# Attention on one core: two matmuls of ones moved ahead of the first transposition, another count of planned matmul work, and new orders for four engines

## The chip, the core and the metric

The kernel runs on one core of one Trainium2 chip. The core has five engines that run side by side, each through its own list of instructions in order: TensorE (PE, matrix products, with weight loads PEld that overlap them), VectorE (DVE), ScalarE (ACT), GpSimd (POOL) and SyncE (SP), whose list here holds the issues of transfers (DMAs). Engines wait for each other through semaphores. The metric is device time in microseconds, the median of the runs of one kernel.

## The reference

32 heads, 2048 positions, 20 elements a head. Queries and keys are normalised to length one, the logits are scaled by one factor a head, and softmax attention follows:

```python
def setup_inputs():
    ...
    B, H, S, D = 1, 32, 2048, 640
    Dh = D // H
    ...
def reference(q, k, v, t):
    eps = 1e-6
    qn = q / (jnp.sqrt((q * q).sum(axis=-1, keepdims=True)) + eps)
    kn = k / (jnp.sqrt((k * k).sum(axis=-1, keepdims=True)) + eps)
    logits = jnp.einsum('bhqd,bhkd->bhqk', qn, kn) * t[None, :, None, None]
    attn = _softmax(logits, axis=-1)
    return jnp.einsum('bhqk,bhkd->bhqd', attn, v)
```

The cost is the 32 x 2048 x 2048 exponentials: the products have only 20 rows or columns, and all data are 16-bit floats.

## The kernel before

**Units.** A head's 2048 x 2048 logits are cut into 64 units of 128 keys by 512 queries. Two paths turn logits into exponentials.

The first is ScalarE's. TensorE puts a *wave* of two or three units into the accumulator psA (L903 for products on 21 rows of the array, two or three side by side; L910 for products on 64 rows, two side by side), and one ACTIVATE (L998) turns the wave into 16-bit exponentials in the ring p_ring. Waves of two and three units alternate in two halves of psA, so TensorE can write one while ScalarE reads the other. There are 1204 such units in 482 waves. ScalarE takes them strictly in their number's order.

The second is VectorE's. TensorE puts four units, as two products on 64 rows (L915), into psF, and one pass on VectorE (L1059) makes of them integers whose two 16-bit halves, read as floats, are rough exponentials. Three shifted copies of that tile (the same integers plus a constant) are made either by VectorE (L1072, L1074) or by GpSimd with a 64-bit addition (L1026, one or two copies a call). The four versions, weighted, average the error away. There are 211 such tiles.

**The second product.** L931 multiplies exponentials with the values, four units side by side, each on 32 columns of the array, and accumulates in psF. A column of ones in the values yields the softmax's denominator. At a head's end VectorE transposes the sum (L947), divides (L956, L960) and a transfer stores it.

**Preparation of a head.** Transfers load q, k and v; VectorE squares and sums (L743, L746), forms the inverse root (L750 to L772) and scales (L791); SyncE issues a transposing transfer into qkT (L817, named trn), and from there copies: three rotated sets of keys kR (six transfers a head, named rot), two into qP for VectorE's path (named qo) and four into qz for L910 (named qz). The loads are named ldq, ldk and ldv, the stores st. All of them share SyncE's one list, up to six heads ahead of their use.

**The first head** is done apart, to begin early. Matmuls of ones (L832) run on TensorE as soon as the ones are written. Eleven of them exist; nine stand ahead of the first transposition of keys (L865, named tk0), two among the first waves. VectorE squares and sums q and k (L730, L733), forms the inverse root and scales (L854, L858). A combination with constants in the query tile (L635), for which GpSimd makes columns (L628 to L632), precedes this on VectorE. TensorE transposes the keys in two halves (L865), ScalarE and VectorE copy them out (L874, L876), and VectorE transposes the queries (L868). Then come the first waves. Twelve further matmuls of ones (L873) stand between the waves of this stage. Their results are overwritten later.

**The order** is written out by hand in the class Program: four lists of task numbers, PE, DVE, POOL and SP, and replay() puts the engines' tasks in that order. In POOL an H stands for one of VectorE's instructions that GpSimd's additions may not run beside; a plus sign begins an addition, with two numbers when one call makes two copies, and an s behind a number in DVE says that VectorE makes that copy in the form of L1072. Behind the lists stands times(), which plays the order through with planned durations (a matmul that starts before PE_REST counts double), and fill(), which goes through the planned times in windows of TICK = 3.41 us. Where the planned matmul work of a window falls under FILL, it puts a further matmul into the longest planned pause of TensorE in it, if one is long enough: ones by ones at the start (L842), zeros by ones into the running sum later (L839, four small ones). The work of a task is counted in columns of a matmul that fills the whole array:

```python
    TICK = 3.41
    FILL = 4200.0
    FGAP = 0.32
    GAP0, EARLYPE = 0.24, 45.0
...
            if load(x) < F:
...
            qk.rows, qk.work = (64, 256.0 * len(us)) if two else (32, 128.0 * len(us))
```

plan_waits() then derives every semaphore wait from the tasks' dependences, so a new order gets its own waits.

Of the kernel before, what the change touches and what calls it, by code (L numbers as in the profile page):

```python
# [79 lines left out]
class Program:  # L80
# [4 lines left out]
    PE_REST = 7.3  # L85
# [7 lines left out]
    PE = """  # L93
# [139 lines left out]
    def add(self, eng, name, fn, dur, deps=(), pri=0.0, lat=0.0, dma=None):  # L233
        t = Task(eng, name, fn, dur, deps, pri, lat, dma)
        self.tasks.append(t)
        return t
# [230 lines left out]
def bass_standalone__qk_norm__prompt_kernel(  # L467
# [7 lines left out]
    B, H, S, D = q.shape  # L475
# [36 lines left out]
    with ExitStack() as es:  # L512
# [51 lines left out]
        add = prog.add  # L564
# [621 lines left out]
```

## Time and profile before

| What | Value |
|---|---|
| Median of 3 runs | 562.19 us (562.02 to 566.7) |
| The profiled execution's own time | 570.37 us |
| Its span | 568.6 us |
| TensorE's mean granted clock in it | 0.982 |
| Busy: PE, DVE, ACT, POOL | 548.4, 546.8, 549.5, 472.8 us |
| Exponentials on ScalarE, L998 | 482, together 546.4 us |
| GpSimd's additions, L1026 | 360 calls, 452.2 us |
| Matmuls put in by fill(): L842, L839 | 2, and 32 in fours |

The profiled execution is a single one, taken beside the three timed ones. A row of a group reads: line, engine, operation, target and sources, count, then busy time and the mean of one in ns, then the idle time of the engine just before these instructions with what ended most of it. In rows in order of time the first two numbers are the start and the length, and the bracket is the pause before. In a table of stretches PEclk is the share of its full clock that TensorE was granted; before the first record of the clock, at 5.81 us, it stands at 1.00.

### The profile page before, as it was taken

The numbers are of one execution on the slowest core, as the hardware profiler recorded it, in microseconds if no ns is written. First come the engines' busy times: TensorE is split into PE (matmuls) and PEld (weight loads), VectorE is DVE, ScalarE is ACT, GpSimd is POOL, SyncE is SP. The second block draws the span as 40 slices with busy tenths as digits, with TensorE's granted clock in tenths as the row PEclk, the third lists the DMA queues.
The fourth block names the chain that finished last, engine by engine and source line by source line (L and its number), as shares of the span: only waits on it lengthen the run. The fifth ranks groups of instructions, "written<-read, shape, count | busy, mean of one in ns | idle before, by whom it ended". The sixth has DMA issues, their size and how long they took to land.

```text
span 568.6 us, 15092 instructions
## 1 busy us (share of the span) xinstructions
PE 548.4 (96%) x6267; PEld 157.8 (28%) x6267; DVE 546.8 (96%) x646; ACT 549.5 (97%) x488; POOL 472.8 (83%) x466
## 2 busy tenths in 40 slices
PE   7999999999999989999999999999999999999997
PEld 2122222222222322222222332223223222223322
DVE  8699999989999999999999999999999999999998
ACT  6699999999999999999999999999999999999995
POOL 6386969799699876988789888798888997989994
PEclk8599999999999999999999999999999999999999
DMA  4436544344334343453433444444254432322100
GB/s 66 61 59 97 65 70 76 59 90 61 59 71 72 65 72 60 70 85 61 74 59 75 74 69 68 71 61 73 61 65 81 65 66 45 57 69 53 29 2 30
DMA packets 196229, 36.47 MB, mean 64 GB/s; under 512 B 171769, under 2 KB 196161, under 8 KB 196161
## 3 DMA queue, kind: packets, MB, share of 16 engines
q1 hardware_dynamic: 196016, 35.43, 38.7%
q8 instruction: 49, 0.80, 0.6%
q14 instruction: 20, 0.16, 0.1%
q10 hardware_dynamic: 144, 0.08, 0.1%
HBM read 7.87 MB, written 2.62 MB: 18 GB/s over the span
## 4 chain that ended last, share of the span: by engine, by line
ACT 70%; PE 20%; DVE 5%; SPq 2%; POOL 2%; issue 1%; DMA 0%; POOLq 0%
ACT p_ring L998 70%; PE psF L931 11%; PE psA L903 3%; PE psF L915 2%; PE psA L910 2%; DVE dx L1059 2%; SPq L567 2%; DVE dx L1072 2%; POOL dx L1026 1%; PE psF L873 1%; DVE oT L947 0%; DMA qP<-qkT 0%; DVE rs_sum L746 0%; DVE o_stage L960 0%; PE psF L832 0%
## 5 line engine op out<-in xcount | busy, mean ns | idle before, releaser
L998 ACT ACTIVATE p_ring<-psA 128x1024 bf16<-128x1024 f32 x482 | 546.4, 1318 | 9.1 <-PE psA L903 8.3
L1026 POOL INT64_ADD dx<-dx x360 | 452.2, 1275 | 86.4 <-DVE qkn L791 27.9
L1059 DVE TENSOR_SCALAR dx<-psF 128x1024 int32<-128x1024 f32 x211 | 256.5, 1216 | 14.3 <-PE psF L915 13.9
L931 PE MATMUL psF<-dx,vph 128*32 128x512 bf16 (+1 forms) x2532 | 221.0, 399 | 0.1
L1072 DVE TENSOR_SCALAR dx<-dx 128x1040 int32<-128x1040 int32 x163 | 198.6, 1225 | 0.8
L931 PE MATMUL psF<-p_ring,vaug 128*32 128x512 bf16 x1204 | 109.0, 386 | 0.1
L903 PE MATMUL psA<-qkT,kR 21*128 21x512 bf16 x639 | 99.5, 390 | 6.6 <-ACT p_ring L998 4.3
L931 PE MATMUL psF<-dx,vaug 128*32 128x512 bf16 (+1 forms) x844 | 82.9, 397 | 0.0
L931 PEld LDWEIGHTS psF<-dx,vph 128*32 128x32 f16 x2532 | 57.0, 95 | 86.5 <-issue 54.5
L910 PE MATMUL psA<-qz,kR 64*128 64x512 bf16 x305 | 62.8, 385 | 2.6 <-ACT p_ring L998 2.3
L915 PE MATMUL psF<-qP,kR 64*128 64x512 bf16 x296 | 58.3, 390 | 1.5 <-DVE oT L947 1.1
L903 PEld LDWEIGHTS psA<-qkT,kR 21*128 21x128 bf16 x639 | 24.2, 91 | 96.4 <-ACT p_ring L998 88.6
L931 PEld LDWEIGHTS psF<-p_ring,vaug 128*32 128x32 bf16 x1204 | 28.8, 95 | 42.9 <-issue 28.5
L903 PE MATMUL psA<-qkT 21*128 21x512 bf16 x177 | 35.9, 393 | 1.7 <-ACT p_ring L998 1.3
L931 PEld LDWEIGHTS psF<-dx,vaug 128*32 128x32 bf16 x844 | 21.3, 95 | 30.0 <-issue 20.2
L910 PEld LDWEIGHTS psA<-qz,kR 64*128 64x128 bf16 x305 | 15.6, 93 | 48.2 <-ACT p_ring L998 32.1
L915 PE MATMUL psF<-qP,qkT 64*128 64x512 bf16 x126 | 24.6, 388 | 1.3 <-DMA qP<-qkT 1.3
L915 PEld LDWEIGHTS psF<-qP,kR 64*128 64x128 bf16 x296 | 14.3, 93 | 38.0 <-DVE dx L1059 14.6
L947 DVE STREAM_TRANSPOSE oT<-psF 128x512 f32<-128x512 f32 x32 | 22.8, 712 | 1.9 <-PE psF L931 1.5
L746 DVE TENSOR_REDUCE rs_sum<-sq 128x64 f32<-128x1280 bf16 (+1 forms) x17 | 23.0, 1351 | 0.1
L910 PE MATMUL psA<-qz,qkT 64*128 64x512 bf16 x83 | 19.9, 386 | 0.0
L903 PEld LDWEIGHTS psA<-qkT 21*128 21x128 bf16 x177 | 8.6, 91 | 28.0 <-ACT p_ring L998 24.9
(71 smaller groups left out, 147.2 us busy)
## 6 DMA issues: line engine op xcount, KB each, us to landing
kR<-qkT SPq DMA_DIRECT2D x62, 96.0 KB, 2.2
kR<-qkT SPq DMA_DIRECT2D x62, 64.0 KB, 2.0
qk_sb<-in_k_dram SPq DMA_DIRECT2D x32, 80.0 KB, 2.3
vaug<-in_v_dram SPq DMA_DIRECT2D x32, 80.0 KB, 3.5
out_dram<-o_stage SPq DMA_DIRECT2D x32, 80.0 KB, 1.9
qk_sb<-in_q_dram SPq DMA_DIRECT2D x124, 20.0 KB, 2.5
qz<-qkT SPq DMA_DIRECT2D x104, 21.0 KB
qP<-qkT SPq DMA_DIRECT2D x62, 32.0 KB, 1.9
```

Source lines behind the costliest of these rows:

```text
L567: return add(eng, name, lambda e, tk: e.dma_start(dst, src), dur, deps, pri, lat=lat, dma=key)
L746: sums.append(dv("sum", lambda e, tk, i=i, m2=m2, src=src: e.tensor_reduce(rs["sum"][:, 2 * R * i:2 * R * i + m2], src, AXIS_X, ALU.add), ...
L873: warm.append(add("PE", "warm", lambda e, tk: e.matmul(psO[0], ones[:, 0:128], ones[:, :], start=True, stop=True), PE_MM, [tk_], -198))
L903: return eng.matmul(dst, k_of(h, c, (rho - g) % 4, ps), qkT[h % NT][ps, 0:512], tile_position=(32 * g, 0))
L910: return eng.matmul(dst, k_of(h, c, (rho - g) % 4, ps), qz[h % NZ][ps, g % 2, :], tile_position=(64 * b, 0))
L915: return eng.matmul(dst, k_of(h, c, dl, ps), qP[h % NT][ps, :], tile_position=(64 * b, 0))
L931: last = eng.matmul(psO[h % 2][32 * g:32 * g + 32, :], w_of(g), rhs_of(g), start=start, stop=False, skip_group_check=True, tile_position=( ...
L947: trO[h] = add("DVE", f"tr{h}", lambda e, tk: e.transpose(oT_all[:, so, :, :].rearrange("p r d -> p (r d)"), psO[h % 2]), 0.63, [lambda: p ...
L998: act[w] = add("ACT", f"exp{w}", lambda e, tk: e.activation(p_ring[:, p0 * 512:p0 * 512 + n], psA[:, slot * WAVES[0] * 512:slot * WAVES[0] ...
L1026: return lambda e, tk: e.int64_add(rows(1), rows(0), PHASE_W[c - 1] * 0x100000001)
L1059: return add("DVE", name, lambda e, tk: e.tensor_scalar(dst[:, o + 2 * w0:o + 2 * (w0 + n)].bitcast(I32), psF[:, prog.pair_of[j] + w0:prog ...
L1072: return e.tensor_scalar(gapped(be).bitcast(I32)[:, :, 0:PAD], dx[:, bx:bx + TILE].bitcast(I32), float(PHASE_W[i]), None, ALU.add)
```

## The change

- PE_REST, up to which planned matmuls count double, goes from 7.3 to 6.0 us.
- The first transposition waits for all eleven first matmuls of ones, and the list has all eleven ahead of it.
- A unit of a three-row wave (L903) counts 84 instead of 128 columns in fill(): 512 columns on 21 of 128 rows. The products themselves stay as they are.
- The four lists are new. Tasks are the same, but for one shifted copy that moves from VectorE (162 instead of 163 in the form of L1072) to GpSimd (460 copies in 352 calls instead of 459 in 360). They were planned with transfers that land later than those assumed for the old ones.

In the new lists the head of the kernel reads as follows. TensorE: eleven of ones, the two halves of the transposition, wave 1, wave 0, the first product for VectorE's path, then waves and ones. VectorE: the memsets, with two moved behind the combination of L635 and one moved ahead of the ones, the same chain up to the copy L876, then the qP product and the first tile's L1059 ahead of the second head's squares. SyncE: the same first eight issues, then the three transposing transfers of the first head in a row.

```diff
-    PE_REST = 7.3
+    PE_REST = 6.0
...
     PE = """
-84 83 81 86 80 82 78 79 85 109 110 235 120 237 117 115 282 240 113 121 242 88 245 122 114 118 112 248 291 119 87 250 116 111 300 253 244 256 309 252
...
+87 82 81 86 79 88 83 80 84 85 78 109 110 237 235 282 121 240 118 120 114 242 245 122 119 112 117 248 291 115 250 116 300 253 113 111 256 290 287 244
...
+0 8 4 43 55 9 76 10 95 98 97 99 100 101 102 103 105 106 107 108 124 134 61 283 144 145 146 147 148 93 149 150 92 151 94 152 60 292 286 301 294s 310
...
+H 45 5 44 H 6 49 51 3 H 52 27 46 50 48 53 47 54 H H H 56 H H H H 7 H 57 19 H H H H 58 H H 35 20 66 59 28 36 67 21 72 11 29 H H H 37 73 30 62 68 22 38
...
-            tk1 = add("PE", "tk0", lambda e, tk: tmm(e, psA[:, 2048:2560], kx[:, 0:512], 0, 2), 0.15, [nk1, z_id] + warm[:9], -201)
+            tk1 = add("PE", "tk0", lambda e, tk: tmm(e, psA[:, 2048:2560], kx[:, 0:512], 0, 2), 0.15, [nk1, z_id] + warm[:11], -201)
...
-            qk.rows, qk.work = (64, 256.0 * len(us)) if two else (32, 128.0 * len(us))
+            qk.rows, qk.work = (64, 256.0 * len(us)) if two else (32, 84.0 * len(us))
```

More of the change, by code (lines that the diff above doesn't have):

```diff
@@ L160 @@
-695 686 696 685 697 684 698 833 699 700 834 701 916 925 918s 1070 899s 1079 1088 1097 964 1106 965 1115 933 966 1124 1091s 1177 1090s 1186 1107s 1195
-1126s 1204 967 1117s 1188s 1213 1132 1197s 1179s 1222 968 940 969 1133 970 942 971 1134 972 941 973 1472 974 975 1231 1215s 1278 1279s 1287 1281s 1296
-1225s 1305 1239 1280s 1306s 1314 1297s 1323 1324s 1332 1326s 1388 1473 1397 1398s 1406 1340 1407s 1415 956 1341 955 1342 957 1424 1426s 1433 1425s
-1578 1427s 1587 1581s 1596 1579s 1441 1474 1605 1597s 1614 1475 1623 1476 1477 1449 1478 1450 1479 1448 1480 1481 1482 1632 1617s 1685 1635s 1626s
@@ L164 @@
-1694 1640 1686s 1703 1641 1986 1483 1712 1706s 1721 1715s 1730 1987 1739 1642 1786 1733s 1795 1742s 1804 1747 1787s 1813 1814s 1822 1796s 1831 1823s
-1840 1832s 1841s 1893 1988 1464 1465 1463 1902 1894s 1848 1989 1911 1990 1849 1991 1920 1992 1912 1993 1850 1929 1923s 1938 1932s 1947 1949s 2097
-1950s 2106 1955 2115 2107s 2124 1994 1963 1995 1962 1996 1997 2108 2133 2136s 2142 2126s 2193 2145s 2202 2195s 2150 1964 2151 2205 2211 2494 2152 2220
-2214s 2229 2221s 2238 2230s 2247 2294 2248s 2303 2297s 2312 2255 2495 2321 2306 2330 2322s 2339 2332s 2348 2340s 2401 2349s 2496 2410 2497 2419 2356
@@ L168 @@
-2498 2357 2499 2358 2428 2421s 2437 2413s 2446 2430s 2455 2439s 2605 2449s 2614 2458s 2616s 2463 2500 1977 2501 1978 2502 1979 2503 2623 2504 2632
-2625s 2641 2634s 2650 2642s 2651s 2701 2505 3002 2710 2658 3003 2719 2712s 2728 2722s 2737 2487 2470 2659 2485 2472 2660 2486 2730 2471 2746 2738s
-2755 2756s 2804 2758s 2813 2763 2822 2816s 2831 2815s 2840 2823s 2849 2843s 2858 2850s 2909 2859s 2918 3004 2919 2927 2866 2929s 2936 2939s 2945 3005
-2954 3006 2867 3007 2868 3008 2979 3009 2978 3010 2963 2957s 3108 2966s 2948s 3117 2971 3126 3118s 3135 3128s 3144 3011 2980 3013 3012 3153 3138s 3162
@@ L176 @@
-3501 3932 3941 3915s 3950 3944s 3959 3933s 4011 3961s 4020 3960s 4029 3967 4012s 4038 4023s 4047 4041s 4056 4117 4049s 4126 4050s 4135 4144 4064 4138s
+0 8 4 43 55 9 76 10 95 98 97 99 100 101 102 103 105 106 107 108 124 134 61 283 144 145 146 147 148 93 149 150 92 151 94 152 60 292 286 301 294s 310
+284s 319 172 173 174 142 175 143 176 171 177 141 178 293 179 180 285s 295s 374 383 385s 392 327 401 410 206 419 207 519 208 197 209 328 210 329 211
+198 212 170 169 213 199 214 528 421 537 522s 546 531s 555 539s 427 548s 564 547s 567s 556s 615 624 616s 633 627s 626s 572 443 642 444 651 445 434 446
@@ new lines @@
+447 573 448 436 449 435 450 574 451 660 654s 669 670s 770 773s 779 771s 788 677 781s 797 693 806 694 815 824 825s 880 826s 889 890s 898 883s 907 832
+695 696 833 697 685 698 686 699 684 700 834 701 916 925 1070 899s 1079 918s 1088 1097 964 1106 965 1115 933 966 1124 1090s 1091s 1177 1126s 1186 1117s
+1195 967 1107s 1204 1197s 1188s 1213 1132 1179s 1222 968 969 1133 970 942 971 940 972 941 973 1134 974 975 1472 1231 1215s 1278 1225s 1287 1279s 1296
+1281s 1305 1239 1280s 1314 1306s 1323 1473 1332 1324s 1307s 1388 1326s 1397 1398s 1406 1340 1407s 1415 1341 956 1342 1424 1426s 1433 1425s 1578 1427s
@@ new lines @@
+1587 1581s 1596 1579s 1441 957 955 1474 1605 1597s 1614 1475 1623 1476 1450 1477 1478 1479 1480 1448 1481 1449 1482 1632 1617s 1685 1626s 1694 1687s
+1640 1686s 1703 1641 1483 1986 1712 1706s 1721 1715s 1730 1987 1739 1642 1786 1733s 1795 1742s 1804 1747 1787s 1813 1814s 1822 1796s 1831 1832s 1840
+1824s 1893 1841s 1988 1902 1894s 1848 1989 1911 1990 1962 1991 1465 1849 1992 1464 1993 1912 1920 1463 1850 1994 1929 1923s 1938 1932s 1947 1949s 2097
+1950s 2106 1955 2115 2107s 2124 1995 1963 2108 1964 1997 1996 2133 2136s 2142 2135s 2193 2145s 2202 2195s 2150 2494 2205 2151 2211 2152 2220 2214s
@@ new lines @@
+2229 2221s 2238 2247 2230s 2294 2248s 2303 2297s 2312 2255 2321 2330 2322s 2339 2332s 2495 2348 2340s 2349s 2401 2496 2410 2497 2419 2356 2498 2357
+2499 2358 2500 1977 2501 2428 2421s 2437 2413s 2446 2430s 2455 2439s 2605 2458s 2614 2449s 2616s 2463 2502 1979 1978 2503 2623 2504 2632 2625s 2641
+2634s 2650 2642s 2651s 2701 2471 2505 3002 2710 2658 3003 2719 2712s 2728 2722s 2737 2472 2470 2659 2746 2738s 2755 2758s 2756s 2804 2660 2731 2487
+2486 2813 2763 2822 2816s 2831 2815s 2840 2823s 2849 2843s 2858 2850s 2909 2859s 2918 3004 2919 2927 2866 2929s 2936 2939s 2945 3005 2954 3006 2867
@@ new lines @@
+3007 2978 3008 2485 3009 2868 3010 2963 2948s 2957s 3108 2966s 3117 2971 3126 3128s 3135 3118s 3144 3011 2979 3012 3013 3153 3138s 3162 3147s 3218
+3156s 3227 3165s 3236 3170 3229s 3245 3238s 3254 3171 2980 2995 2994 2993 3172 3263 3257s 3312 3248s 3321 3313s 3330 3271 3504 3339 3331s 3348 3505
+3357 3366 3340s 3417 3350s 3426 3360s 3435 3419s 3444 3374 3428s 3453 3438s 3462 3447s 3471 3456s 3506 3598 3464s 3474s 3607 3601s 3479 3507 3616 3508
+3488 3509 3375 3510 3511 3486 3512 3487 3513 3376 3514 3625 3627s 3634 3618s 3643 3644s 3652 3653s 3708 3709s 3717 3660 3719s 3726 3735 3729s 3744
@@ L177 @@
+3738s 3753 3661 3515 3662 3800 3809 3755s 3818 3761 3812s 3827 3801s 3836 3845 3821s 3854 3830s 3905 3855s 3914 3846s 3923 3862 3863 3502 3503 3501
+3932 3941 3915s 3950 3944s 3959 3933s 4011 3961s 4020 3960s 4029 3967 4012s 4038 4023s 4047 4041s 4056 4049s 4117 4050s 4126 4135 4144 4064 4138s
 4136s 4153 4156s 3864 4119 4154 4065 4155 4066 4161 4162 4163
@@ L184 @@
-+644 +652 +662 +661 +672 +653v,663v +671 453 +772 +782 +780 +790 +789 H +798 463 +799 +791,800 +808,817 +807,816 +809 +818 +827 +882 +881 +892 +891 H
-H H H H H H H H H H H +910 +900 +908 +926,917 +901 +909 +927 +1072 703 +919 H +928 +1073 +1082 +1080 H +1081,1099 717 +1089,1071 +1098,1116 +1127
-+1108 +1125 +1118,1109 +1100v,1196 +1205 +1178 +1180,1189 +1206v,1187 H H H H H H H H H H H H H H +1198 +1223 +1207v,1232 +1234,1216 +1233 +1224 977
-+1214 991 +1298 +1288 +1290,1308 +1289 +1316,1307 +1315,1299v +1317 +1334 +1325 +1333 +1389,1335v +1391,1400 +1390,1399 +1408 H H H H H +1417 1005
@@ L192 @@
-+2213,2222 +2223,2232 1999 +2239 +2231 +2250,2241 +2249,2240 +2296,2305 2013 +2295,2313 +2304 H +2323 +2324 +2315 +2331,2314v +2341 +2333,2342 +2351 H
-+2403,2350 +2402,2411 2027 H H H H +2404 +2420,2412v +2422,2431 +2429 +2448 +2438 +2456,2447 +2440 +2457 +2607 +2606,2615 2041 H H H H H H H +2617 H
-+2626 +2624 +2608,2635 +2643 +2633 +2644 +2653 +2652 H H +2704 +2702 +2713 +2703 2507 +2720 +2711 +2729,2721v H H H H H H H H H +2731 +2740 +2748
-+2739 +2749v,2747 +2757 +2806 +2807v,2805 +2825 +2814 +2824 +2834 +2832 +2841 +2842,2833 +2852 2521 +2851 +2860 +2912 +2861 H H +2910,2920v +2928
@@ L196 @@
-+2921v,2911v +2930 +2938 +2946,2937 H H H H H H H H H +2947,2956 +2965 +2964,2955 +3111 +3109 2535 +3110 +3119 +3129,3120 +3127,3136 H H H H +3145
-2549 +3155,3137 +3154,3146v +3164 +3219,3163 +3230 3015 +3220v,3228 +3239,3221 +3237,3246 H H H H H +3256 +3255 +3266 +3247 +3265 +3264 +3322 +3314
-3029 H +3333 +3332,3341 +3315,3324 +3323v,3349 +3342 +3369 +3358 +3367 +3351 +3368 +3359v,3427 +3420 +3429 3043 +3446 +3436,3418 +3455 +3437
-+3445,3463 +3454 H +3465 +3473 +3472 +3599 +3608 +3610 +3600v,3609v H H H H H H H H H H H H +3619 3057 +3628 +3617,3626 +3635 +3636 +3646 +3637 +3655
@@ new lines @@
+12 74 23 64 70 31 75 65 24 13 69 H 25 32 33 126 14 34 39 125 71 63 128 127 129 40 15 H H H H H H H H H H H 41 16 42 H 130 +303 +304 +312 +302 154 H 17
++320 H H H H H H H H H H H 26 H 18 +313 +322 +321v,311 +376 +375 +384 +386 182 +393 +377 +403 H +411,402 +394,412 H H H H H H H H H H H H H H +395 H
++404 +422 +413v,420 +520,529 216 +521 +558 +538 +557 +540 +530 +565 +549 226 +618 +617 +566 +625 +636 +635 H +634 +645 +643 H H H H H H H H H H H H
++644 +652 +653,662 +663,672 +671,772 +661 +780 +782 453 +791 +790 H +789 463 +798,807 +799,808 +817 +827 +800 +881,818v +809 +816 +892 +891,882 H H H
@@ new lines @@
+H H H H H H H H H +910 +909 +917 +926 +908 +901 +900 +928 703 +919 +927 H +1080 +1071,1089 +1081 H +1100 +1072v,1098 +1073 717 +1082v,1125 +1109
++1099,1108 +1180,1127 +1189 +1118 +1205,1116 +1178,1187 +1196,1206v H H H H H H H H H H H H H H +1216,1198 +1223,1207v +1232,1214 +1224,1233 977 +1234
+991 +1288,1297 +1289 +1308,1299 +1298v,1315 +1317,1290 +1335 +1333,1316v +1325 +1334,1390 +1400,1391 +1389 +1399,1408 H H H +1417 +1409 +1418v,1416
++1436 +1434 1005 +1435 +1580 +1588 +1589 +1598 1019 H H H +1599,1590 +1606 +1608 +1607v,1615 H H H H H H H H H H +1624,1616v +1634,1625 +1635 +1633
@@ new lines @@
++1696 +1697 +1688 1485 H H H +1704 +1714 +1705v,1713 +1722,1695 +1723 +1732 H +1724v,1731 +1741 +1740 +1788 +1798,1789 +1797,1806 +1815 +1805,1807v
++1816 +1823 +1834 +1825 +1842,1833 +1843 1499 H +1895 +1904 1513 +1896v,1903 +1905 H H H H H H H H H +1913 H H H +1921 +1914 +1922v,1930 +1939 +1941
++1931,1940 +1948 +2099 +2098 +2100,2109 +2116 1527 H H H H H H +2127,2118 +2126,2117 +2143 +2144 +2134,2125 +2196 +2194 H H H +2203 H 1999 +2204,2213
++2212 +2222 +2231 +2232 +2239,2223v +2249,2240 +2250v,2241v +2305,2296 +2314 +2315 +2304,2295 +2323 +2306 2013 +2313,2324v +2333,2342 +2341 +2331
@@ new lines @@
++2351 H +2350 +2403 +2411,2402 H H H H H H H 2027 +2412v,2404v +2420,2429 +2431,2422 +2447 +2438 +2440 +2448v,2456 +2607,2457 +2606,2615 2041 H H H H
++2617 H +2626,2608 +2633 +2624 +2643 +2635 +2653 +2644 +2652 H H H +2702 +2711 +2704,2713 +2721 2507 +2703 +2729,2720 H H H +2739,2730 +2747
++2740,2749 +2757,2748 H H H H +2806 +2807 +2805 2521 +2825 +2824 +2834 +2832,2814 +2833v,2841 +2851 +2852 +2860 +2861 +2842 +2911 H H +2912 +2910,2928
++2921,2930 +2920,2938 +2937,2946 H H H H H H H H H +2955,2947v +2965 +2956v,2964 +3110 +3111 +3119 2535 +3109,3120v +3129 +3127,3136 H H H H +3145
@@ new lines @@
+2549 +3154,3146v +3155,3137 +3163 +3220,3164 +3219,3228 3015 +3239,3230 +3237 +3221v,3246 H H H H H H +3255 +3256 +3247v,3264 +3265 +3266 +3322 +3315
+3029 H +3323,3332 +3314 +3333v,3324v +3351 +3341 +3342 +3369 +3358 +3349,3367 +3418,3359v +3368v,3427 +3437 +3445,3436 +3420,3429 +3446 3043 +3463
++3454 +3455 H +3473 +3465 +3472,3599 +3600 +3609 +3610 +3608 H H H H H H H H H H H H +3619 +3617,3626 3057 +3628 +3636 +3635 +3637 +3646 +3654,3645
++3655 +3711 +3710 +3718 +3720 3517 +3727 +3728 +3737 +3736 +3745 +3746 H H H +3756 +3747v,3754 +3802 +3811 +3810 +3820 3531 +3819,3803v +3829 +3828
@@ L204 @@
++3837 +3847 +3839 +3856 +3848 +3838 +3906,3857v +3917 +3908 3545 H H H H +3907 +3925 +3926 +3916 +3943 +3952 +3935 +3951 +3924 +3934 +3942 +3953,3962
++4022 +4013 +4030 +4014v,4021 +4040 +4039,4031v +4048 +4032 +4058 +4057 +4118 +4059 +4120,4129 +4137 +4147 +4127,4145 +4146v,4128v H H H H H H H H
 """
     SP = """
[20 rows of a table removed]
[19 rows of a table added]
 """
```

20 lines of the change are left out of this document (removed), and 157 rows, old and new, of tables (PE, SP).

## The prediction

> **What bounds the kernel now.** I read the head of the page first, then ScalarE's groups, then ScalarE's and TensorE's rows in order of time where ScalarE had pauses, and last a table of stretches for the granted clock.
>
> ```profile
> span 568.6 us, 15092 instructions
> ...
> PE 548.4 (96%) x6267; PEld 157.8 (28%) x6267; DVE 546.8 (96%) x646; ACT 549.5 (97%) x488; POOL 472.8 (83%) x466
> ...
> L998 ACT ACTIVATE p_ring<-psA 128x1024 bf16<-128x1024 f32 x482 | 546.4, 1318 | 9.1 <-PE psA L903 8.3
> ```
>
> Three engines stand at 96 to 97%, but only ScalarE (ACT) has a row that cannot shrink: 482 exponentials, 546.4 us, the same count after the change. The span is therefore: time to the first exponential, 546.4, pauses between exponentials, and what follows the last one. ScalarE's rows in order of time give all four:
>
> ```profile
> 8.09 2.37 ACT L998 ACTIVATE p_ring<-psA 128x1024 bf16<-128x1024 f32 x2 [0.98 <-PE psA L903]
> 10.65 1.02 ACT L998 ACTIVATE p_ring<-psA 128x1024 bf16<-128x1024 f32 x1 [0.20 <-PE psA L903]
> 12.16 2.37 ACT L998 ACTIVATE p_ring<-psA 128x1536 bf16<-128x1536 f32 x2 [0.49 <-PE psA L903]
> 15.61 1.45 ACT L998 ACTIVATE p_ring<-psA 128x1536 bf16<-128x1536 f32 x1 [1.07 <-PE psA L903]
> 17.65 1.02 ACT L998 ACTIVATE p_ring<-psA 128x1024 bf16<-128x1024 f32 x1 [0.59 <-PE psA L903]
> 19.70 2.37 ACT L998 ACTIVATE p_ring<-psA 128x1536 bf16<-128x1536 f32 x2 [1.03 <-PE psA L903]
> 22.96 1.45 ACT L998 ACTIVATE p_ring<-psA 128x1536 bf16<-128x1536 f32 x1 [0.90 <-PE psA L903]
> 24.90 1.02 ACT L998 ACTIVATE p_ring<-psA 128x1024 bf16<-128x1024 f32 x1 [0.48 <-PE psA L903]
> 26.75 5.97 ACT L998 ACTIVATE p_ring<-psA 128x1536 bf16<-128x1536 f32 x5 [0.83 <-PE psA L903]
> ```
>
> ```profile
> 207.83 2.37 ACT L998 ACTIVATE p_ring<-psA 128x1536 bf16<-128x1536 f32 x2 [0.18 <-PE psA L903]
> 210.72 1.45 ACT L998 ACTIVATE p_ring<-psA 128x1536 bf16<-128x1536 f32 x1 [0.52 <-PE psA L903]
> 212.66 1.02 ACT L998 ACTIVATE p_ring<-psA 128x1024 bf16<-128x1024 f32 x1 [0.49 <-PE psA L910]
> 214.73 1.45 ACT L998 ACTIVATE p_ring<-psA 128x1536 bf16<-128x1536 f32 x1 [1.04 <-PE psA L903]
> ...
> 560.59 1.94 ACT L998 ACTIVATE p_ring<-psA 128x1024 bf16<-128x1024 f32 x2 [0.22 <-PE psA L910]
> ```
>
> The exponentials begin at 8.09 us. The brackets from 10.65 to 26.75 add up to 0.20+0.49+1.07+0.59+1.03+0.90+0.48+0.83 = 5.59 us, those at 207.83 to 214.73 to 2.23, the last to 0.22: 8.04 in all. The last exponential ends at 562.53, so 6.07 us follow it. 8.09 + 546.4 + 8.04 + 6.07 = 568.6. The profiled execution took 570.37, 1.77 outside the span. All pauses wait for TensorE (PE), and the clock says why:
>
> ```profile
> core 0: us, PE busy (x) PEld busy (x) DVE busy (x) ACT busy (x) POOL busy (x), PEclk, DMA share, GB/s
> 5.81:9.22 3.41, 2.24 (x14) 0.78 (x14) 3.11 (x9) 1.52 (x3) 2.76 (x15) 1.00 0.58 36
> 9.22:26.29 17.07, 17.07 (x77) 3.15 (x75) 11.97 (x22) 11.93 (x10) 6.24 (x16) 0.50 0.54 70
> 210.61:214.02 3.41, 3.41 (x31) 0.76 (x28) 3.29 (x3) 2.47 (x2) 3.41 (x4) 0.50 0.47 96
> 371.03:374.45 3.42, 2.52 (x29) 0.73 (x27) 3.40 (x5) 3.42 (x4) 3.32 (x3) 1.00 0.60 43
> ```
>
> TensorE ran at half its clock from 9.22 to 26.29 us and from 210.61 to 214.02: 17.07 us and 3.41 us, five times 3.41 and once. Both losses lie in ScalarE's pauses above. The window just before the first fall was thin: 14 matmuls, busy 2.24 of 3.41. Its groups on TensorE:
>
> ```profile
> L873 PE MATMUL psF<-ones 128*128 128x512 bf16 x3 | 1.0, 386 | 0.0
> L903 PE MATMUL psA<-qkT 21*128 21x512 bf16 x5 | 0.8, 385 | 0.3 <-DVE qkT L868 0.3
> L842 PE MATMUL psF<-ones 128*128 128x256 bf16 (+1 forms) x2 | 0.7, 370 | 0.0
> L865 PE MATMUL psF<-ident,p_ring 128*128 128x128 bf16 x2 | 0.3, 224 | 0.2 <-DVE p_ring L854 0.2
> L865 PE MATMUL psA<-ident,p_ring 128*128 128x128 bf16 x2 | 0.3, 224 | 0.7 <-DVE p_ring L854 0.7
> ```
>
> I weigh each by its columns times the share of the 128 by 128 array that it fills: 3x512 + 5x512x21/128 (420) + 256 + 4x128 = 2,724, and up to 512 for the last matmul of L842, which straddles 9.22: 2,724 to 3,236. The same sum for 371.03 to 374.45, a thin window that kept its clock, comes, cut at its edges, to about 4,050. The level that decides lies between.
>
> The three times shown are 562.19 (median), 562.02 and 566.7. 570.37 less all 8.04 of pauses is 562.33. So I read the median as an execution with next to no pauses, and 566.7 as one that had most of the first fall (4.5 of 5.59). This is the point on which the forecast turns: **the median already stands at the floor of this order.**
>
> **The change part by part.**
>
> *Two more matmuls of ones ahead.* They are not new: two of the eleven stand today behind the fourth and the sixth waves, where the filling step must now make up 512 columns each. The nine that stand ahead take:
>
> ```profile
> 1.69 4.02 PE L832 MATMUL psF<-ones 128*128 128x512 bf16 x9 [1.69 <-DVE ones L570]
> ...
> 7.66 0.39 PE L903 MATMUL psA<-qkT 21*128 21x512 bf16 x2 [0.34 <-DVE qkT L868]
> ```
>
> That is 4.02 / 9 = 0.45 us each. VectorE's (DVE) and ScalarE's rows beside them:
>
> ```profile
> 0.88 0.09 DVE L652 MEMSET t<- 128x32 f32 x1 [0.88 <-PEq L1171]
> 0.94 0.14 DVE L570 MEMSET p_ring<- 128x96 f32 x1
> ...
> 1.66 0.38 DVE L570 MEMSET p_ring<- 128x384 uint32 x1
> 2.12 0.11 DVE L612 MEMSET p_ring<- 128x64 bf16 x1
> ```
>
> ```profile
> 6.72 0.38 ACT L874 ACTIVATE qkT<-psA 128x256 bf16<-128x256 f32 x1 [1.02 <-PE psA L865]
> ```
>
> In the new VectorE list the memset of 0.38 stands ahead of the ones instead of those of 0.09 and 0.14, so the matmuls begin at about 1.69 + 0.15 = 1.84. Eleven end at 1.84 + 11 x 0.45 = 6.79 if none runs fast, 0.4 behind the start of the first transposition today (6.72, less the 0.32 to the copy, is 6.40). That is hidden: the first logits wait for VectorE's transposition (qkT L868), not for this one; ScalarE's copy ended at 7.10 and the logits began at 7.66, so 0.56 us is spare. Were it not, 0.4 would be added. What the two bring is work in the window that decides: at the profile's phase about two fall after 5.81, some 1,000 columns.
>
> *Counted work 128 to 84 a unit.* Nothing in the computation changes; the filling step puts matmuls of ones or zeros into planned pauses where planned work falls under 4,200 a window. It now sees the three-unit waves of L903 at 252 instead of 384. Today it has put in two on L842 and eight on L839 (32 matmuls in fours). At the trace's own phase four windows beyond the fall at 207 come out under 4,200, so I estimate 4 to 15 more. A four costs 0.22 us of TensorE. With none hidden that is 0.9 to 3.3 us; with all hidden, 0. I take 0: they stand in pauses where TensorE waits for ScalarE anyway, which the 347.5 us stretch below shows to be most of its waits.
>
> ```profile
> L998 ACT ACTIVATE p_ring<-psA 128x1536 bf16<-128x1536 f32 (+1 forms) x307 | 347.5, 1315 | 1.3 <-PE psA L903 1.0 <-PE psA L910 0.2
> ```
>
> From 216 us to the end 307 exponentials wait 1.3 us in all, 1.04 of it the tail of the fall. TensorE's slack is real there. If the cover went, each filler would come straight onto the chain.
>
> *Order at the start.* Wave 1 now stands ahead of wave 0 on TensorE, while ScalarE still takes wave 0 first. Both become ready together at 7.66. Wave 0 is late by one set of row tiles: nothing if they overlapped, 0.45 at half clock; I take 0.22, about half of it, since the clock was full then (385 ns for one in the row of L903 above). On VectorE the row of L635 starts the chain that leads to 7.66:
>
> ```profile
> 2.85 0.32 DVE L635 SCALAR_TENSOR_TENSOR p_ring<-p_ring 128x80 bf16<-128x80 f32 x1 [0.62 <-POOL p_ring L632]
> ...
> 3.24 0.33 DVE L730 TENSOR_TENSOR sq<-qk_sb 128x320 bf16<-128x320 bf16 x1
> ```
>
> Two memsets (L612's 0.11 and L652's 0.09) move from ahead of it, where the 0.62 of waiting hid them, to behind it: +0.20. GpSimd (POOL) has a shorter memset in place of a longer one ahead of the selects of L632, which gives back at most about as much. Between 0 and +0.20; I take +0.06, nearer to nothing. The first exponential: 8.09 + 0.22 + 0.06 = 8.37. The first tile's L1059 (1.22 us) moves ahead of the second head's normalisation; a memset of 0.5 goes behind it. That head is first used some seventeen waves of about 1.2 us later, so it costs nothing; without that cover, 0.7.
>
> *Steady state.* VectorE loses one of its 646 instructions, a shifted copy that GpSimd takes over; GpSimd makes 460 additions in 352 calls instead of 459 in 360. ScalarE waits for neither in the 347.5 us above: nothing. The transfers are as many as before.
>
> *Transfers.* The fall at 210.61 begins here:
>
> ```profile
> 207.97 1.19 SPq L567 DMA_DIRECT2D qP<-qkT  x2
> ```
>
> ```profile
> 209.96 0.39 PE L915 MATMUL psF<-qP,qkT 64*128 64x512 bf16 x2 [1.28 <-DMA qP<-qkT]
> ```
>
> The second copy into qP of head 11 was issued 40 places behind that head's transposition on SyncE's (SP) queue, behind loads for heads 17 and 18; it now stands 30 behind. At 1.19 / 2 = 0.6 us an issue that is 6 us sooner, more than the 1.3 us by which it was late. Over all heads the last qP copy moves from 23.5 places behind to 21.8, the last of kR from 22.7 to 23.0: some are nearer, some farther. A wait elsewhere of the same kind would cost up to the same 2.2 us; none costs nothing. I take nothing.
>
> *The end.* Behind the last logits TensorE works through its left-over products without a break:
>
> ```profile
> 560.81 4.20 PE psF L931 x65
> ```
>
> Both lists have 18 such groups there, and VectorE's last passes are the same. No change.
>
> **Sum.** Against the profiled execution: 570.37 - 5.59 (first fall gone) - 2.23 (second gone) + 0.28 (start) = 562.83. Against the median, which I take to have neither: 562.19 + 0.28 = 562.47. **Forecast 562.5**, own range 561.7 to 563.3.
>
> [...]
>
> **The rivals.**
>
> *The first fall stays* (the other side: slower). If in most executions the window behind the release still holds less than about 3,200 of weighed work, TensorE goes to half clock for five windows, and ScalarE pauses 4.5 to 5.6: 562.5 + 4.5 to 5.6 = 567.0 to 568.1. For it: the phase of the windows is not the kernel's to choose, and one execution of the three shown, and the profiled one, had it. Against it: by my count the new head holds 1,000 (ones) + 512 + 420 + 512 (first pair of L915) + 1,000 or more in the window that now holds 2,724 to 3,236. Chance 0.14.
>
> *The change does not do what it says.* If the clock goes by long pauses alone, neither the ones nor the fillers matter and the fall comes as often as before: 562.5 where it stays away, 567 where it comes. [...] Chance 0.04, half for each time.
>
> *Fillers on the chain.* Ahead of the 4.20 us TensorE has left-over work. Fillers there, or in planned pauses that do not exist on the chip, delay the end one for one: 0.9 to 3.3 us, 563.4 to 565.8. Chance 0.10.
>
> *The median was not at the floor.* If executions outside the profiler still have pauses, up to 1.5 us could go: 561.0 to 561.7, a little less if the start doesn't slip. Chance 0.12. More than that would need fewer exponentials.
>
> **How the numbers follow.** The forecast has 0.60. A measurement of this kernel tells about 1% (5.6 us) from no change. Faster than 556.6 would leave 556.6 - 1.77 - 546.4 = 8.4 us for start and end, which take 8.09 + 6.07 today: 0.01. Slower than 567.8 takes some third of the first rival and what joins others: 0.06. Same: 0.93. The range leaves out most of the first rival: 560.9 to 566.3.
>
> **What would show it.** First exponential at 8.3 to 8.4; first wave of L903 with three ahead of two; a clock of 1.00 from the release on, no stretch at 0.50 near 9 to 26; ScalarE's pauses behind the first exponential under 1 us; L839 well above 32; span near 560.7. A pause of ScalarE above 1 us at a DMA, or half clock for more than one window, makes the prediction wrong.

## The result, and the profile after

| | Median | Lowest to highest | Runs | Profiled execution |
|---|---|---|---|---|
| before | 565.79 us | 562.02 to 569.72 | 21 | 570.37, span 568.6 |
| after | 562.23 us | 562.14 to 562.99 | 21 | 562.15, span 560.4 |

The ratio after to before is 0.9943, 95% interval 0.9924 to 0.9963. (Ratios here are formed from fast runs alone, those within 1.5% of a kernel's fastest, and are not the quotient of the two medians.) The change makes the kernel 0.57% faster, and the form of the gain is in the spread: the fastest run of before, 562.02, lies below every run of after, but only four of before's 21 runs lie below 563, against all 21 of after. The median of 562.19 that the prediction started from came from the first three of the 21 runs.

The page of the changed kernel, its head and ScalarE's exponentials:

```profile
span 560.4 us, 15135 instructions
...
PE 541.9 (97%) x6294; PEld 157.3 (28%) x6295; DVE 545.2 (97%) x645; ACT 548.7 (98%) x488; POOL 472.6 (84%) x458
...
L996 ACT ACTIVATE p_ring<-psA 128x1024 bf16<-128x1024 f32 x482 | 545.6, 1323 | 1.3 <-PE psA L901 1.0 <-PE psA L908 0.2
```

(The lines are two lower than before: L998 is now L996, L903 is L901, L865 is L863, L839 is L837, L842 is L840.) The idle time ahead of the exponentials went from 9.1 us to 1.3. ScalarE's rows in order of time, the first stretch and the last exponentials:

```profile
7.09 0.38 ACT L872 ACTIVATE qkT<-psA 128x256 bf16<-128x256 f32 x1 [1.38 <-PE psA L863]
8.29 23.88 ACT L996 ACTIVATE p_ring<-psA 128x1024 bf16<-128x1024 f32 x21 [0.82 <-PE psA L901]
...
552.40 1.94 ACT L996 ACTIVATE p_ring<-psA 128x1024 bf16<-128x1024 f32 x2 [0.24 <-PE psA L908]
```

Where before had eight pauses up to 26.75, there is now one row of 21 exponentials in which the view shows no break. The last exponential ends at 554.34 and 6.09 us follow. TensorE's rows at the start, and the windows around the release of its clock, at 7.54 in this execution:

```profile
1.96 4.88 PE L830 MATMUL psF<-ones 128*128 128x512 bf16 x11 [1.96 <-DVE ones L568]
6.63 0.42 PE L863 MATMUL psA<-ident,p_ring 128*128 128x128 bf16 x2
6.92 0.40 PE L863 MATMUL psF<-ident,p_ring 128*128 128x128 bf16 x2
7.10 0.60 PE L840 MATMUL psF<-ones 128*128 128x512 bf16 x1
7.64 0.61 PE L901 MATMUL psA<-qkT 21*128 21x512 bf16 x5
```

```profile
core 0: us, PE busy (x) PEld busy (x) DVE busy (x) ACT busy (x) POOL busy (x), PEclk, DMA share, GB/s
4.13:7.54 3.41, 3.41 (x12) 1.19 (x10) 3.14 (x10) 1.18 (x3) 2.79 (x31) 1.00 0.49 49
7.54:10.95 3.41, 3.17 (x17) 0.82 (x17) 3.26 (x6) 2.66 (x3) 2.90 (x12) 1.00 0.74 71
```

TensorE is busy 3.41 of 3.41 us ahead of the release and 3.17 behind it, where before had 2.24 in the window that was followed by half clock. Weighed as in the prediction, with matmuls cut at the windows' edges, the two hold by my estimate about 4,030 and 4,680 columns; before's window from 5.81 holds 3,100 by the same sum. Note that the clock column says 1.00 for 4.13 to 7.54, although the matmul of L840 at 7.10 took 0.60 us: the record of the clock begins with the first release. I come back to that.

### The profile page after: what moved, and what is told of

Same layout as the page of the kernel before. It is cut to its first block, busy times and chain, and to the rows that moved or that the text cites. A ratio compares the mean times of both kernels' runs of the same rounds, so it can differ in the third digit from the quotient of the medians.

```text
span 560.4 us, 15135 instructions
## 1 busy us (share of the span) xinstructions
PE 541.9 (97%) x6294; PEld 157.3 (28%) x6295; DVE 545.2 (97%) x645; ACT 548.7 (98%) x488; POOL 472.6 (84%) x458
## 4 chain that ended last, share of the span: by engine, by line
ACT 84%; PE 15%; DVE 0%; issue 0%
ACT p_ring L996 84%; PE psF L929 9%; PE psA L901 2%; PE psF L913 2%; PE psA L908 2%; PE psF L830 1%; DVE oT L945 0%; DVE ones L568 0%; DVE o_stage L958 0%; PE psF L840 0%; DVE p_ring L568 0%; DVE rec L954 0%; PE psF L863 0%; PE psA L863 0%; DVE act_scr L568 0%
## 5 line engine op out<-in xcount | busy, mean ns | idle before, releaser
L996 ACT ACTIVATE p_ring<-psA 128x1024 bf16<-128x1024 f32 x482 | 545.6, 1323 | 1.3 <-PE psA L901 1.0
L929 PE MATMUL psF<-p_ring,vaug 128*32 128x512 bf16 x1204 | 107.3, 382 | 0.1
L901 PE MATMUL psA<-qkT,kR 21*128 21x512 bf16 x639 | 98.2, 385 | 7.1 <-ACT p_ring L996 5.2
L901 PEld LDWEIGHTS psA<-qkT,kR 21*128 21x128 bf16 x639 | 24.1, 91 | 95.8 <-ACT p_ring L996 88.6
L929 PEld LDWEIGHTS psF<-p_ring,vaug 128*32 128x32 bf16 x1204 | 29.0, 94 | 42.7 <-issue 27.6
L901 PE MATMUL psA<-qkT 21*128 21x512 bf16 x177 | 35.1, 384 | 0.8 <-ACT p_ring L996 0.3
L901 PEld LDWEIGHTS psA<-qkT 21*128 21x128 bf16 x177 | 8.5, 91 | 26.1 <-ACT p_ring L996 24.0
```

The source lines that it names most:

```text
L901: return eng.matmul(dst, k_of(h, c, (rho - g) % 4, ps), qkT[h % NT][ps, 0:512], tile_position=(32 * g, 0))
L929: last = eng.matmul(psO[h % 2][32 * g:32 * g + 32, :], w_of(g), rhs_of(g), start=start, stop=False, skip_group_check=True, tile_position=( ...
L996: act[w] = add("ACT", f"exp{w}", lambda e, tk: e.activation(p_ring[:, p0 * 512:p0 * 512 + n], psA[:, slot * WAVES[0] * 512:slot * WAVES[0] ...
```

## The experiments

Each kernel was timed in five rounds beside the kernel before. Before had a median of 567.87 us in the session of e1, e2, e4 and e5, 566.36 in that of e3, e6, e7 and e8, and 566.22 in that of e9 to e12, so small differences are safest within a session.

| Kernel | Order | Ones ahead | Fill: count, put in | Median | Lowest to highest | Ratio to before |
|---|---|---|---|---|---|---|
| e1 | old | 9 | 84, 14 | 565.66 | 562.38 to 569.17 | 0.9996 (0.9958 to 1.0034) |
| e2 | old | 11 | 128, 11 | 563.66 | 562.21 to 570.23 | 0.9979 (0.9946 to 1.0011) |
| e3 | old | 11 | 84, 17 | 562.62 | 561.71 to 568.39 | 0.9944 (0.9909 to 0.9979) |
| e9 | old, new transfers | 11 | 84, 20 | 565.24 | 564.08 to 566.81 | 0.9991 (0.9963 to 1.0018) |
| e5 | new | 11 | none | 564.74 | 562.85 to 573.69 | 0.9976 (0.9936 to 1.0016) |
| e10 | new | 11 | 84, start only, 6 | 563.20 | 562.22 to 564.28 | 0.9959 (0.9929 to 0.9988) |
| e4 | new | 11 | 128, 12 | 563.20 | 562.47 to 563.52 | 0.9946 (0.9914 to 0.9978) |
| e12 | new | 11 | 128, 12 | 562.23 | 561.99 to 563.42 | 0.9959 (0.9933 to 0.9986) |
| e7 | new | 9 | 84, 19 | 562.33 | 562.10 to 562.54 | 0.9938 (0.9908 to 0.9967) |
| e8 | new, wave 0 first | 11 | 84, 19 | 562.76 | 562.14 to 564.19 | 0.9949 (0.9919 to 0.9978) |
| e11 | new | 11 | 84 to 5600, 40 | 562.54 | 562.35 to 564.75 | 0.9952 (0.9920 to 0.9983) |
| e6 | after | 11 | 84, 20 | 562.25 | 562.10 to 562.61 | 0.9936 (0.9904 to 0.9968) |

### The parts of the change in the old order: e1, e2, e3

e1, the count alone:

```diff
-            qk.rows, qk.work = (64, 256.0 * len(us)) if two else (32, 128.0 * len(us))
+            qk.rows, qk.work = (64, 256.0 * len(us)) if two else (32, 84.0 * len(us))
```

> The old order and nine ones ahead; only the count of a three-row unit goes from 128 to 84, which puts in four fours of zeros more (14 put in instead of 10; one of the four before 45 us). Theory A (the fall of the clock in the first 30 us makes the spread of before, and the window around the release decides it): next to nothing near the release has changed, so the median stays at 565.8 within 1 us and the spread stays 562 to 570. Theory B (the counted fill of the pauses holds the clock): median near 562.5, spread under 1.5 us. Theory C (late transfers, cured by the new order): 565.8, as A.

565.66, spread as before: the count alone does nothing that these runs show. The one filling that it adds ahead of 45 us stands behind 15 us and not at the release. Theory B, in the form that the count does it, falls. The trace of this run (569.17 us) holds a trap for the reader. Two stretches, and two groups of the first one:

```profile
9.00:27.60 18.60, 18.60 (x85) 3.55 (x82) 11.75 (x22) 12.47 (x11) 6.47 (x16) 1.00 0.51 65
27.63:31.05 3.42, 3.32 (x42) 0.83 (x34) 3.25 (x7) 2.72 (x3) 1.28 (x3) 1.00 0.30 79
```

```profile
L903 PE MATMUL psA<-qkT,kR 21*128 21x512 bf16 x15 | 3.6, 603 | 0.0
L903 PE MATMUL psA<-qkT 21*128 21x512 bf16 x10 | 2.4, 604 | 0.0
```

The clock reads 1.00, yet the products of these groups took 603 ns, as in the half-clock stretch of before, and not 385. Here TensorE was not released until 27.63; the record starts there. Weighed as above, its windows from 3.74 and from 7.15 held only 2,810 and 2,550 columns. So the loss has two forms: a release that is followed by a fall (before's trace) and a release that comes late (e1's). In both traces it ends behind a window of more than 3,200 by the same sum (3,210 in before, from 22.88; 3,220 in e1), and both cost ScalarE's pauses: 5.6 us in before, 6.8 here.

e2, the ones alone in the old order (the two numbers leave their places among the waves):

```diff
-84 83 81 86 80 82 78 79 85 109 110 235 ...
+84 83 81 86 80 82 78 79 85 88 87 109 110 235 ...
...
-    PE_REST = 7.3
+    PE_REST = 6.0
...
-            tk1 = add(... [nk1, z_id] + warm[:9], -201)
+            tk1 = add(... [nk1, z_id] + warm[:11], -201)
```

> The old order, but all eleven ones ahead of the first transposition (and PE_REST 6.0); the count stays 128. 11 matmuls put in instead of 10. Theory A: the release comes in time whatever the phase of the windows and the window behind it is thicker by 1,000, so the median falls to 562.2 to 563.5 and the mean clock to 0.99 or better in nearly all runs. Theory B: no change, 565.8. Theory C: no change, 565.8.

563.66, just above Theory A's 563.5, with single runs up to 570.23, and the interval of the ratio reaches 1. The runs shift all the same: ten of twelve lie below 564.6, against seven of before's 35 in that session. Most of what Theory A says, with something left over. e3 adds the count of 84 to it:

> The old order with both local parts of the change: eleven ones ahead and the count of 84 (17 matmuls put in, 10 of them before 45 us). If ones and fill are all there is to it: 562.3 to 562.8 and a spread under 1.5 us. If the new order (later landings) has a share of its own: single runs still fall, median 563 to 564.5, highest above 566, as with the ones alone (563.66, highest 570.23).

562.62: the two together bring seven of twelve runs below 563, but five lie between 563.17 and 568.39. The median is that of the first alternative, the highest run that of the second. Its trace (564.07 us) shows what is left. TensorE in order of time, the stretches, and a step of the chain of waits:

```profile
32.43 0.39 PE L903 MATMUL psA<-qkT,kR 21*128 21x512 bf16 x2
34.01 0.39 PE L915 MATMUL psF<-qP,kR 64*128 64x512 bf16 x2 [1.19 <-DMA kR<-qkT]
34.33 0.60 PE L903 MATMUL psA<-qkT,kR 21*128 21x512 bf16 x5
35.72 0.54 PE L915 MATMUL psF<-qP,qkT 64*128 64x512 bf16 x2 [0.79 <-DVE dx L1059]
```

```profile
32.41:35.83 3.42, 1.44 (x15) 0.42 (x11) 2.27 (x4) 2.82 (x3) 2.30 (x4) 1.00 0.57 52
35.83:39.24 3.41, 3.41 (x29) 0.70 (x27) 2.84 (x3) 2.29 (x3) 1.82 (x1) 0.50 0.45 53
```

```profile
30.05 3.83 DMA kR<-qkT
```

A copy into kR is issued at 30.05 and lands 3.83 us later. TensorE waits 1.19 for it and 0.79 for VectorE behind it, the window is busy 1.44 of 3.42, and the clock falls for one window; ScalarE pauses 2.2 us in all. e2's trace has the same fall, at 35.4. The traces of before and e1 have not: there the first loss held TensorE back by 5.6 and 6.8 us, and the copy had landed when it was needed (in before it is issued at 33.30, and the product at 37.24 does not wait for it). **A wait stood hidden behind the first loss and came out when that was cured.** The changed kernel has a pause of 0.18 us at 33.51 in that place.

### The transfers alone: e9

e9 is e3 with SyncE's list taken from the new order.

> Old order with the eleven ones and the count of 84, and SyncE's list alone from the new order (20 matmuls put in). In the old order with both local parts TensorE paused 1.19 us at 34 us for a copy into kR (issued at 30.05, landed 3.83 us later) and 0.79 behind it, and the clock fell at 35.8. If the order of the transfers is what the new order brings: that pause is gone, no fall at 35, median 561.9 to 562.3, highest under 563.5. If the later first use on the other engines is needed: falls as before, median 562.5 to 563.2, single runs at 563 to 564 and above.

565.24, both alternatives missed: the first was faster, and the second put the median at 562.5 to 563.2. The copy into kR is issued at 30.57 here and still late, the clock falls at 36.61, and the chain of waits has loads of q (2.36 us at 146.66, 3.91 at 211.21) and of k (2.38 at 242.79). So the new list of transfers brings nothing in the old order of the other engines. Which of the other three lists brings the new order's share, none of these runs separates.

### The fill in the new order: e5, e10, e4, e12, e11

e5 puts nothing into the pauses:

```diff
-    FILL = 4200.0
+    FILL = 0.0
```

> The new order and eleven ones with nothing put into the pauses at all (0 instead of 20). Theory A: the ones and the order alone hold it, 562.2 to 563. Theory B: the first fall comes in most runs, 565 to 568. Theory C: 562.2 to 563. If the 20 put in cost anything on the chain, this one is below 562.2.

564.74 and up to 573.69: just under Theory B's 565 to 568, and no run of it is as fast as the slowest of the changed kernel's second timing (e6, 562.61). Ones and order do not hold the clock by themselves; Theory A in the form "the ones alone" falls too. Its trace falls like before's; the last line is a thin window, later on, that keeps the clock:

```profile
5.55:8.97 3.42, 2.08 (x15) 0.56 (x12) 3.17 (x9) 1.23 (x3) 2.80 (x19) 1.00 0.62 38
8.97:15.79 6.82, 6.82 (x23) 1.37 (x21) 5.14 (x16) 5.63 (x6) 1.44 (x9) 0.50 0.52 90
...
244.48:247.90 3.42, 2.10 (x25) 0.52 (x21) 3.42 (x4) 3.42 (x3) 3.32 (x4) 1.00 0.19 41
```

e10 keeps the fill in windows that begin ahead of 12 us: six matmuls of ones, no zeros.

```diff
-            if load(x) < F:
+            if x < 12.0 and load(x) < F:
```

> The changed kernel with the fill only in windows that begin ahead of 12 us: the 6 matmuls of ones, none of the 14 fours of zeros. If the start alone decides (no fill at all gave 562.85 to 573.69): 562.2 to 562.6 with no run above 563.5. If the later fours hold the clock too: single runs with a fall behind 12 us, highest above 564, clock under 0.998 in them.

563.20, between both: no run has a mean clock below 0.999 or takes more than 564.28, so none has a fall, and none the 5 to 7 us of the early losses. The six keep those away. But eleven of twelve runs stay 0.6 to 2.1 us above 562.2. The profiled execution took 562.22 and shows nothing of the others' loss. A release that comes somewhat late need not show in the mean clock (e1's profiled execution took 569.17 us, with a release at 27.63 and a mean clock of 1.0); the cause stays open.

e4 and e12 are one kernel, the new order counted with 128:

> The new order and eleven ones, but counted with 128: 12 matmuls put in instead of 20, 8 instead of 12 before 45 us. Theory A: 562.2 to 562.6, as after. Theory B: falls return in some runs, median 563 to 566. Theory C: 562.2 to 562.6.

> The new order counted with 128 once more, beside a chip of its own session. It had 562.47 to 563.52, and its trace a pause of 0.83 us at 251.8 that came from a late load of v. If that was the chip: 562.2 to 562.5 here. If the 8 fewer matmuls put in cost it: 563 again, without late loads.

563.20 the first time, 562.23 the second, with seven of twelve runs at 561.99 to 562.25 and five at 563.17 to 563.42. In e4's trace 0.83 us of pause come at 251.84 from a load of v:

```profile
243.43 3.49 DMA vaug<-in_v_dram
```

The second median speaks for something in the first session, such as late loads, and against the count; five runs above 563, of which no trace was kept, don't let me call that settled. In the new order 12 or 20 fillings make at most 0.2% of difference.

e11 doubles what is put in (FILL 5600):

> The changed kernel with FILL at 5600: 40 matmuls put in instead of 20. It prices what is put in. Hidden, as the prediction took it: 562.2 to 562.4, nothing lost. On the chain (the rival): 20 more at 0.22 us give up to 4.4 us, 563 to 566.6.

562.54, lowest 562.35 against e6's 562.10: in seven runs (562.35 to 562.59) the 20 more cost about 0.25 us, 0.01 us each, not 0.22. A group of its trace (124 matmuls, where the changed kernel has 56):

```profile
L837 PE MATMUL psF<-ones,nil x124: 376/379/392, 19.7 to 482.6; 128*32 128x512 bf16 x124
```

In these runs they are hidden, as the prediction took it. The other five of twelve are at 563.26 to 564.75, two of them with a mean clock of 0.997, as e2's trace has it with its one fall. The trace kept (563.26) has a late release, at 8.00 (one matmul of ones of L840 took 634 ns, against 379 in the median), and pauses of 0.36 in all at 247.5 and 252.3. What makes these five slower stays open.

### The ones and the first waves in the new order: e6, e7, e8

e6 repeats the changed kernel beside e3, e7 and e8:

> The changed kernel itself, beside the next three on one chip. Theory A+B (the eleven ones see to the release in time and the fill, counted by rows, holds the clock behind it): 562.2 to 562.6, spread under 1 us. If the 563.2 of the new order counted with 128 came from the chip of that session (late transfers) and not from the fewer fillings, this one comes out near 563 too when it falls on a chip like that.

562.25, as before. e7 has nine ones ahead and two among the waves again:

```diff
-87 82 81 86 79 88 83 80 84 85 78 109 110 ... 242 245 122 ... 291 115 250
+82 81 86 79 83 80 84 85 78 109 110 ... 242 88 245 122 ... 291 87 115 250
...
-            tk1 = add(... [nk1, z_id] + warm[:11], -201)
+            tk1 = add(... [nk1, z_id] + warm[:9], -201)
```

> The new order and the count of 84, but nine ones ahead and two among the first waves, as before (19 matmuls put in, 12 before 45 us). If the ones decide the release (Theory A): for phases in which no window ahead of about 6.5 us holds enough, TensorE stays at half clock until 15 to 28 us, so some 20 to 40% of the runs lie 2 to 6 us above 562.2 and the median at 562.3 to 565. If the new order and fill alone are enough: 562.2 to 562.6 with no run above 563.5.

562.33, no run above 562.54: the eleven are not needed here. TensorE's rows tell why:

```profile
1.96 3.65 PE L830 MATMUL psF<-ones 128*128 128x512 bf16 x9 [1.96 <-DVE ones L568]
6.38 0.29 PE L863 MATMUL psA<-ident,p_ring 128*128 128x128 bf16 x2 [0.78 <-DVE p_ring L852]
6.51 0.59 PE L840 MATMUL psF<-ones 128*128 128x512 bf16 x2
```

With the two gone the fill has put two (L840) between the transpositions, where the changed kernel has none. Ones by hand and ones by the fill replace each other: in e7's trace the window ahead of its release, at 5.10, holds 3,790 columns and the one behind it 3,800. In before the fill had put one of 256 columns there (L842 in the window quoted with the prediction). e7 does without the eleven and e12 without the count of 84; the new lists without either, the four lists alone, were not run.

e8 puts wave 0 ahead of wave 1 again (237 235 to 235 237 in TensorE's list):

> The changed kernel with wave 0 ahead of wave 1 on TensorE again (19 matmuls put in). The step of the prediction that put 0.22 us on the swap: the first exponential comes 0.2 to 0.4 us sooner and the median falls to 561.9 to 562.1. Rival (the first exponential waits for something else, or the fill is disturbed): 562.2 to 562.6 or more.

```profile
8.04 25.44 ACT L996 ACTIVATE p_ring<-psA 128x1024 bf16<-128x1024 f32 x22 [1.07 <-PE psA L901]
```

The first exponential comes at 8.04 instead of 8.26 in e6, as priced, and yet the spans are 560.51 and 560.45: the exponentials take up the lead in small pauses, 0.70 us in all against 0.47 (0.14 of it at 15.89). The median is 562.76, but the spans of the twelve runs have the same median, 560.5, as e6's; most of the difference lies outside the span. The 0.22 is real at the start and buys nothing at the end. No kernel of this study has a median below that of the changed one.

## Why the prediction was wrong, point by point

**The step that failed is "the median already stands at the floor of this order".** The time came as forecast (562.23 against 562.5), but no gain was forecast, and before's median is 565.79. The floor itself was rightly sized (562.33 and 562.47 in the prediction); that two of the first three runs stood near it was the luck of the draw. I took them for the rule, although the profile in hand had the fall and the two sums differed by it: against the profiled execution I took 5.59 for the first fall, against the median nothing. Of before's 21 runs only four lie below 563. Whether the loss comes goes, as I read the traces, with where the windows lie, as the rival "the first fall stays" itself said, and that differs from run to run: the changed kernel was released at 7.54 in one execution (after, its eleven ones taking 4.88 us) and at 4.69 in another (e6, its eleven ones taking 3.88). How often a loss of this kind comes can't be read from three draws. The term was 0 of 5.59 and measured 3.6 between the medians (565.79 to 562.23).

**The mechanism was right, but for one of two forms of the loss.** The windows of 3.41 us, which fill() assumes, can be read off before's trace: its stretches of the clock from 5.81 on last 3.41, 17.07, 184.32 and 3.41 us, which is 1, 5, 54 and 1 times 3.413. In the traces the first fall goes with a thin window behind the release, the work weighed by the part of the array that it fills: e5 takes the fill away and the fall is back. Three executions, whose windows behind the release begin at nearly the same time, show it side by side: with 2,660 columns (e5, from 5.55) and 3,100 (before, from 5.81) the clock fell, with 3,600 (e8, from 5.68) it held. The prediction had no term for the other form, a release that comes late (e1). It is not rare: in e1's session 24 of before's 35 runs take 564.6 to 570 us, and 14 of these have a mean clock of 0.999 or 1.0, as e1's trace has.

**The level** was put between the 2,724 to 3,236 of the thin window and 4,050. By the traces, sums cut at the windows' edges: half clock followed 3,100 and 2,550 (before), 1,360 (e3), 2,660 (e5), 2,280 (e2) and 2,610 (e9); full clock was kept after 3,070 (e5, at 244.48) and 3,190 (e8, at 32.99); TensorE was released after 3,150 (e5), 3,210 (before) and 3,220 (e1) and was not after 2,980 (before), 3,090 (e1, from 13.98) and 3,180 (e11, from 1.18). e9 was released after 2,940; why is not shown. From these sums I estimate one level near 3,100, with an error of some 150, for fall and release; the estimate is for these traces alone.

**Two more ones ahead.** They begin at 1.96, not 1.84, and ScalarE's copy began at 7.09, 0.37 later than before. In the profiled execution, at half clock until 7.54, they are not hidden as worked out. Its chain of waits runs through them, the transposition and a filling to the first logits:

```profile
1.96 4.88 PE psF L830 x11
6.84 0.21 PE psA L863 x2
7.05 0.26 PE psF L863 x2
7.31 0.39 PE psF L840
7.71 0.56 PE psA L901 x4
```

In e6, released at 4.69, the first logits wait for VectorE's transposition, as worked out:

```profile
7.61 0.61 PE L901 MATMUL psA<-qkT 21*128 21x512 bf16 x5 [0.21 <-DVE qkT L866]
```

The price is small: the first exponential comes at 8.29 and at 8.26. What the two bring shows in the old order (e2, in the share of good runs, not clear of noise in the ratio) and is nothing beside a fill that does the same (e7).

**The count.** 4 to 15 more expected, 10 put in by the change as a whole; hidden in most runs, as taken (e11). Alone the count shows no effect (e1).

**The start.** The swap was priced at 0.22 and measured 0.25 to 0.22 (8.29 and 8.26 to 8.04), but it doesn't reach the end (e8). The +0.06 on VectorE measured -0.03 (its row of L728 begins at 3.21, before 3.24).

**The transfers: "I take nothing".** For the changed kernel this held: ScalarE's pauses behind the first exponential are 0.48 us in all. Overlooked was what the new lists had to prevent: in the old order, with the first loss cured, a late copy at 30 us makes a fall of its own, 2.2 us (e3). I looked only for transfers that were late in before's trace, and there this one was covered by the fall. The 2.23 of the second fall, which was put down to a late copy into qP, was not lasting either: e1, e2 and e3 keep the old list of transfers, and none of their traces has a wait for that copy or a fall near 210. So its absence after the change is not shown to come from the new list.

**Sum against the profiled execution:** 562.83 forecast, 562.15 measured. Start 8.29 (-0.08), exponentials 545.6 instead of 546.4 (-0.8; traces with other pauses have 545.5 in e3 to 546.2 in e5, and why is not shown), pauses 0.48 instead of 0.22 (+0.26), the end 6.09 (+0.02), the rest outside the span.

**The rival "the change does not do what it says".** It needs a clock that goes by long pauses alone. The runs speak against that. Before's longest pause in the window ahead of its first fall is this one:

```profile
6.40 0.28 PE L865 MATMUL psA<-ident,p_ring 128*128 128x128 bf16 x2 [0.69 <-DVE p_ring L854]
```

e5's window ahead of the fall has no pause above 0.56 us, and e1's TensorE, without any pause from 9.0 to 27.6 us, stayed at half clock. Plain busy time does not decide either: the clock fell after 2.24 us of 3.41 (before) and held after 2.10 of 3.42 (e5, from 244.48).

## What to carry to other kernels

Where a loss depends on a phase that the kernel doesn't choose, three runs say little about how often it comes: when the profile has a loss that the timed median lacks, forecast with its share, not without it. Here it paid to weigh thin stretches of TensorE by the rows and columns that the products fill, and to pad them, above all around the first release (564.74 us with nothing put in, 563.20 with the six at the start, 562.25 with all twenty); what is put into real pauses cost little, about 0.25 us for twenty more in the good runs of e11. When one loss is cured, look for the wait that stood behind it, since the trace of before can't show it.

## What the runs showed that I had not expected

- TensorE can be busy without a break and still be held at half clock: before for 17.07 us, e1 from 9.0 to 27.6 us, 18.60 of 18.60 busy, 603 ns a product. That products on 21 rows or on 32 columns count by their part of the array is my estimate from the sums above: before was not released behind a window busy for 3.41 us of 3.41 with 2,980 columns (from 12.64), and was behind one busy as long with 3,210 (from 22.88).
- The granted clock reads 1.00 ahead of its first record, and a run's mean clock leaves that time out: e1's run of 569.17 us has a mean clock of 1.0. The lengths of single matmuls (385 or 603 ns) tell what the clock was.
- A first exponential that comes 0.22 us sooner left the span as it was.
